# A gated scan and feed-forward kernel: interleaved head rows, state products in two column parts, and a planner with other transfer costs

## The chip, the cores and the metric

The kernel runs on one core of one Trainium2 chip. The metric is device time of one execution in microseconds (us), the median of several runs. A difference of about 0.2% is what these runs can tell from no change.

## What is computed

Per batch (4) and head (8) a complex state of 48 x 48 is carried over 768 steps: it is decayed by a complex gate, a product of key and value is added, and the query reads its real part. Then every token goes through a feed-forward block with a quadratic unit in between.

```python
mag = np.sqrt(a_re * a_re + a_im * a_im)
scale = np.minimum(mag, 0.999) / (mag + 1e-06)
for t in range(S):
    new_re = ar * S_re - ai * S_im
    new_im = ar * S_im + ai * S_re
    S_re, S_im = (new_re + kv, new_im)
    y[:, :, t] = np.einsum('bhd,bhde->bhe', q[:, :, t], S_re)
...
h = x @ w_in                                       # 3072 x 384 by 384 x 2048
g = np.where(pos, h, np.where(neg, 0.0, (h + beta) ** 2 / (4.0 * beta)))
return (g @ w_out).astype(np.float32)
```

## The kernel before

**Units and blocks.** The 4 x 768 tokens are cut into 12 units of 256 tokens (`U`); a batch is three units. Two units make a block; there are six blocks. Per block the feed-forward part (`moe`) works on 512 tokens: 16 steps `f`, each with 9 matmuls into `h` (L951) and, three steps later, 9 into the outputs `o` (L1026); in between ACT and DVE form `s`, `g`, `gh` and `gl`. Each product of two float32 values is made of three fast matmuls, of a high part with a high part, a low part with a high part and a high part with a low part.

**Gates.** `gates(u)` computes, on DVE and ACT alone, the running sum of the logarithm of the gate's size and of its angle along the tokens (scans at L544 and L571). Key and query (`kq`) are scaled by it (L561) and multiplied by the cosine into `x` and by the sine into `kq` itself (L647, the helper `turn`). In these tiles the partitions are rows of several heads.

**Spreading the heads.** The matmuls want all 96 rows of one head (48 cosine, 48 sine) in one tile. `spread` moves them by DMAs from SBUF to SBUF into three head tiles, `hd0` to `hd2`, with five transfers for the cosine rows and five for the sine rows of a unit: 48, 48, 32, 16 and 16 partitions. The order of the rows in `x` comes from `key_rows`, which the host uses to lay out the inputs: 48 rows of one head, then 48 of another, and so on; the cosine rows go to partitions 0 to 47 of the head tile, the sine rows to 48 to 95. There is one set of head tiles for all units but unit 1.

**Attention.** `attend(u)` takes a unit as two chunks of 128 tokens and makes, per chunk: scores (`sc`, L791, masked by DVE into `am`, L799), transposes of the keys (`tp`, L737, copied by ACT to `kT`), state products (`dp`, L764: per head one matmul of 128 tokens, 96 columns of `kT` loaded, 48 columns of values moving; DVE adds them to the state `st`, L774 and L776), and values (`yp`, L830 from the state, L838 from `am`: two heads go side by side into columns 0 to 63 and 64 to 127 of the array). ACT copies `yp` to `xr` and `ys`, and six small DMAs (`xr<-ys`) bring the rest rows of a block into place before the block is split into `xH` (ACT, L921) and `xL` (DVE, L928).

These steps are put together in *visits*: the parts of one visit follow each other on PE without anything between, and the first of them waits for the inputs of all. Per chunk the visits are: values of the chunk before and both groups of scores; then state products of the chunk before and transposes. The last visit of a unit has state products, then values.

**Weights.** Each of 16 weight tiles comes packed (`raw_i`, `raw_o`) and is unpacked by three DVE instructions (L377, L386, L395) and an ACT cast to the high part (L401). The low part is a DVE subtraction (L406), but for the first `LO_PE` = 4 tiles it is made by PE (L415, L416) and copied by ACT (L430).

**The order of the work.** Every operation is recorded with an engine, a cost, its reads and writes and perhaps a due time (`Plan.op`). `Plan.order` then plays the plan with these numbers: each engine takes, among the operations that are ready, the one due first. The result is written out engine by engine and not changed at run time. A DMA costs `DMA_ISSUE` = 70 ns of SP, starts 1500 ns later, moves 260 bytes per ns one after the other, and its end is seen 900 ns later. All DMAs are issued by SP, in one order; each uses one of eight semaphores in turn, and waits until the transfer that had it before is finished. Attention of the units of block `b + 1` is due in a stretch of the feed-forward part of block `b`, given by `WINDOW` (and `EARLY` for the first). Units 0, 1 run before the first feed-forward part. Where PE would stand idle in the start, `warm` adds matmuls without use (`idle`, L1075).

Of the kernel before, what the change touches and what calls it, by code (L numbers as in the profile page):

```python
# [20 lines left out]
NH = 8  # L21
S = 768
D = 48
DM = NH * D
DFF = 2048
# [30 lines left out]
LAG = 3  # L56
HOLD = {'DVE': (0.3, 20000.0), 'ACT': (0.3, 20000.0)}
WINDOW = (0.05, 0.7)
EARLY = (0.05, 0.6)
HEAD = ((15000, 8000), (8000, 2000))  # L60
# [3 lines left out]
WARM = 0.75  # L64
ABS_ACT = 5
LO_PE = 4
INFLATE = 1.6
# [40 lines left out]
class Plan:  # L108
# [42 lines left out]
    def order(self):  # L151
# [8 lines left out]
        for i in range(n - 1, -1, -1):  # L160
            eng, cost, _, _, d, dma = ops[i]
            t = big if d is None else d
            if dma:
                own = DMA_FIX + DMA_END + dma / DMA_BW + 600
# [11 lines left out]
        avail = {e: [] for e in free}  # L176
        dma_free = 0.0

# [9 lines left out]
        while done < n:  # L188
# [105 lines left out]
def gated_scan_moe(  # L294
# [55 lines left out]

    def dma(nbytes, dst, src, r=(), w=(), due=None):
        return pl.op(
            "SP", DMA_ISSUE, lambda: nc.sync.dma_start(dst(), src()), r=r, w=w, dma=nbytes, due=due  # L353
        )
# [9 lines left out]
    def weights(n, kind, i, slot):  # L364
# [7 lines left out]
        N = 2 * DM  # L372
        pl.op("SP", DMA_ISSUE, lambda: load(k, RAW.get()), w=[RAW], dma=P * N * 8)
        pl.op(
# [60 lines left out]
    def ranges(k):  # L435
        RAW = tl(turn_of("g", 4), [P, 2 * DM, 2], U32, f"chk_{k}")
        top, low = (lambda: RAW.get()[:, :, 1]), (lambda: RAW.get()[:, :, 0])
        N = 2 * DM
        pl.op("SP", DMA_ISSUE, lambda: load(k, RAW.get()), w=[RAW], dma=P * N * 8)
# [26 lines left out]
    def gates(u):  # L466
# [158 lines left out]
        if u == 1:  # L625
# [3 lines left out]
                    "hd_1",  # L629
                    lambda t, n=n: t[: 2 * D, : 2 * n * U].rearrange(  # L630
                        "p (j e n) -> p j e n", j=n, e=2
# [4 lines left out]
        else:  # L636
            hd = [
                tl(f"hd{g}", [2 * D, n, 2, U], F32, f"hd_{u}_{g}")
                for g, n in enumerate((3, 3, 2))
            ]  # L640
# [16 lines left out]
        def spread(g, e, t):  # L657
            r = D * e
            h = hd[g]
            row = 2 * U * 4  # L660
            if g < 2:
                dma(
                    D * NJ * row,
                    lambda: h.get()[r : r + D],
                    lambda: t.get()[g * D : (g + 1) * D],
                    r=[t],
                    w=[(h, e)],
                )
            else:
                dma(  # L670
                    64 * row,
                    lambda: h.get()[r : r + 32],
                    lambda: t.get()[2 * D :, 0:2],
                    r=[t],
                    w=[(h, (e, 0))],
                )
                for q in range(2):
                    p = 2 * D + 16 * q
                    dma(
                        16 * row,  # L680
                        lambda q=q: h.get()[r + 32 : r + D, q],
                        lambda p=p: t.get()[p : p + 16, 2],
                        r=[t],
                        w=[(h, (e, 1 + q))],
                    )
# [13 lines left out]
    def attend(u):  # L699
# [28 lines left out]
        def transposes(c):  # L728
            cs = slice(c * CH, (c + 1) * CH)
            out = []  # L730
            for g in range(2):
                TP = bank([P, 4, 2 * D], f"tp_{u}_{g}_{c}")
                KT = tl(turn_of("kT", 2), [P, 4, 2 * D], F32, f"kT_{u}_{g}_{c}")

                def run(g=g, TP=TP):
                    for i, h in enumerate(GROUPS[g]):
                        PE_.transpose(  # L737
                            TP.get()[:, i, :], head(h)[:, 0, cs], ident[: 2 * D, : 2 * D]
                        )

                def tail(TP=TP, KT=KT):
                    pl.op(
                        "ACT",
                        act(8 * D, psum=True),
                        lambda: A_.copy(KT.get(), TP.get()),
# [8 lines left out]
        def products(c):  # L754
            kT = carry.pop("kT")
            DP = bank([2 * D, NH, D], f"dp_{u}_{c}")
            V_c = carry["V"]
            old = carry.get("st")
            ST = tl(turn_of("st", 3), [2 * D, NH, D], F32, f"st_{u}_{c}")
            carry["st"] = ST  # L760

            def run():
                for i in range(NH):
                    PE_.matmul(  # L764
                        DP.get()[:, i, :],
                        kT[i // 4].get()[:, i % 4, :],
                        V_c[0].get()[:, V_c[1], i * D : (i + 1) * D],
                        start=True,
                        stop=True,
                    )  # L770

# [6 lines left out]

            return [(NH * pe32(D), run, [*kT, V_c[0]], DP, tail)]

# [108 lines left out]
        if part == 0:  # L889
            carry.pop("st", None)  # L890
            carry.pop("kT", None)
        for c in range(NC):
# [5 lines left out]
            if part * NC + c < S // CH - 1:  # L898
                second = second + transposes(c)
            if second:  # L900
                visit(second)
            carry["V"] = (V, c)
        last = values(NC - 1, *pending)
        if part < NPART - 1:
            last = products(NC - 1) + last
        visit(last)
# [451 lines left out]
```

## Time and profile before

| | |
|---|---|
| runs shown | 600.36, 600.93, 600.93 us; median 600.93 |
| profiled execution | 598.38 us, span of its instructions 596.6 us |
| granted TensorE clock, mean | 0.982 |
| first feed-forward matmul starts at | 86.34 us |
| last feed-forward matmul starts near | 589 us |

The profile is of one execution. Its rows name a line of the kernel, an engine, an operation and the tiles (out<-in) with their shapes and counts. In the profile a float32 matmul of the attention part counts as two, as PE makes two passes of it; the fast matmuls of the feed-forward part count as one. PEld is the load of a matmul's stationary operand. A matmul's duration includes its way through the array, so in a row of matmuls the pace is read from the starts, not from the durations. SPq is SP issuing DMAs.

### The profile page before, as it was taken

How to read it: one execution, taken by the hardware profiler on the slowest of the kernel's cores; microseconds unless marked ns; L12 is line 12 of the kernel's file. 1: busy time of each engine (PE TensorE's matmuls, PEld its weight loads, DVE VectorE, ACT ScalarE, POOL GpSimd, SP SyncE). 2: the span in 40 equal slices, each digit the busy share in tenths (PEclk: the TensorE clock that was granted, in tenths of full speed). 3: DMA queues.
4: the chain of work that ended last, by engine and by line, in shares of the span. 5: the costliest groups of instructions: out<-in, count | busy, mean ns of one | idle time of the engine just before them, and what ended most of it. 6: DMA issues, size and time to landing. Idle time of an engine off the chain costs nothing.

```text
span 596.6 us, 9075 instructions
## 1 busy us (share of the span) xinstructions
PE 560.9 (94%) x3502; PEld 474.5 (80%) x3502; DVE 449.0 (75%) x636; ACT 392.6 (66%) x632; POOL 1.4 (0%) x16
## 2 busy tenths in 40 slices
PE   5378979999999999999999999999999999999995
PEld 5167968888688888888888888888888888888884
DVE  3999979989979899688697687887785444555552
ACT  8658769988887775666756576566567577543332
POOL 0000000000000000000000000000000000000000
PEclk9599989999999999999999999999999999999998
DMA  8379573673381540540710640710765956010001
GB/s 350 125 186 233 162 194 115 175 276 103 105 213 45 107 134 0 136 152 18 181 60 1 145 148 13 190 48 11 175 217 183 236 200 213 13 55 0 1 0 57
DMA packets 21794, 74.18 MB, mean 124 GB/s; under 512 B 3889, under 2 KB 8497, under 8 KB 21745
## 3 DMA queue, kind: packets, MB, share of 16 engines
q1 hardware_dynamic: 21744, 73.55, 42.2%
q8 instruction: 28, 0.46, 0.3%
q14 instruction: 22, 0.17, 0.1%
HBM read 48.76 MB, written 4.72 MB: 90 GB/s over the span
## 4 chain that ended last, share of the span: by engine, by line
PE 66%; DVE 15%; ACT 7%; DMA 7%; SPq 2%; issue 2%; DVEq 0%; ACTq 0%
PE o L1026 26%; PE h L951 26%; PE sc L791 5%; DMA hd<-kq 4%; PE dp L764 3%; PE yp L830 2%; PE yp L838 2%; ACT ai L500 2%; SPq L353 2%; PE tp L737 2%; DVE x L647 1%; DVE ai L571 1%; ACT x L500 1%; DVE kq L561 1%; DVE g L995 1%
## 5 line engine op out<-in xcount | busy, mean ns | idle before, releaser
L951 PE MATMUL h<-xH,wi 128*128 128x512 f32 x576 | 181.6, 396 | 0.9 <-DVE g L995 0.8
L1026 PE MATMUL o<-gh,wo 128*128 128x512 f32 x576 | 178.9, 392 | 0.1
L1026 PEld LDWEIGHTS o<-gh,wo 128*128 128x128 f32 x576 | 107.2, 188 | 23.1 <-issue 0.7
L951 PEld LDWEIGHTS h<-xH,wi 128*128 128x128 f32 x576 | 105.4, 189 | 22.7 <-DVE g L995 2.1
L995 DVE TENSOR_TENSOR g<-h,s 128x512 f32<-128x512 f32 x96 | 65.9, 687 | 67.3 <-ACT s L976 57.0
L1026 PE MATMUL o<-gl,wo 128*128 128x512 f32 x288 | 112.3, 390 | 1.2 <-DVE gl L1013 1.2
L951 PE MATMUL h<-xL,wi 128*128 128x512 f32 x288 | 112.2, 390 | 0.0
L1009 ACT CAST gh<-g 128x512 fp32r<-128x512 f32 x96 | 59.6, 621 | 70.7 <-DVE g L1003 66.7
L976 ACT ACTIVATE s<-h,cst 128x512 f32<-128x512 f32 x96 | 65.8, 687 | 42.4 <-PE h L951 38.8
L1013 DVE TENSOR_TENSOR gl<-g,gh 128x512 fp32r<-128x512 f32 x96 | 66.1, 689 | 31.4 <-ACT gh L1009 30.7
L1026 PEld LDWEIGHTS o<-gl,wo 128*128 128x128 f32 x288 | 54.1, 188 | 13.2 <-DVE gl L1013 1.7
L951 PEld LDWEIGHTS h<-xL,wi 128*128 128x128 f32 x288 | 54.1, 188 | 11.5
L500 ACT ACTIVATE ai<-ai 128x768 f32<-128x768 f32 x53 | 44.6, 845 | 21.7 <-DMA ai<-in_ari_dram 8.0
L1003 DVE SCALAR_TENSOR_TENSOR g<-s,g 128x512 f32<-128x512 f32 x80 | 55.4, 692 | 2.7
L791 PE MATMUL sc<-hd 96*128 96x128 f32 x384 | 50.3, 283 | 5.1 <-DMA hd<-kq 4.6
L791 PEld LDWEIGHTS sc<-hd 96*128 96x128 f32 x384 | 46.4, 194 | 9.4 <-DMA hd<-kq 5.6
L838 PE MATMUL yp<-am,V 128*64 128x128 f32 x384 | 35.5, 273 | 0.0
L799 DVE TENSOR_TENSOR am<-sc,mask 128x512 f32<-128x512 f32 x48 | 32.0, 684 | 3.9 <-PE sc L791 3.7
L830 PE MATMUL yp<-hd,st 96*64 96x128 f32 x320 | 32.1, 278 | 0.0
L764 PEld LDWEIGHTS dp<-V,kT 128*96 128x96 f32 x320 | 30.1, 165 | 1.8
L500 ACT ACTIVATE x<-x 128x768 f32<-128x768 f32 x24 | 20.3, 846 | 15.0 <-DVE x L544 14.7
L764 PE MATMUL dp<-V,kT 128*96 128x48 f32 x320 | 29.6, 245 | 0.0
(86 smaller groups left out, 629.5 us busy)
## 6 DMA issues: line engine op xcount, KB each, us to landing
chk<-in_wl_dram SPq DMA_DIRECT2D x16, 768.0 KB, 4.4
kq<-in_kq_dram SPq DMA_DIRECT2D x12, 768.0 KB, 5.1
ai<-in_ari_dram SPq DMA_DIRECT2D x11, 768.0 KB, 6.0
hd<-x SPq DMA_DIRECT2D x24, 288.0 KB, 5.1
hd<-kq SPq DMA_DIRECT2D x24, 288.0 KB, 5.8
raw_i<-in_wl_dram SPq DMA_DIRECT2D x8, 768.0 KB, 7.7
raw_o<-in_wl_dram SPq DMA_DIRECT2D x8, 768.0 KB, 4.4
V<-in_v_dram SPq DMA_DIRECT2D x12, 384.0 KB, 4.0
```

The source lines that it names most:

```text
L500: lambda: A_.activation(out(), src(), f, **kw),
L764: PE_.matmul(DP.get()[:, i, :], kT[i // 4].get()[:, i % 4, :], V_c[0].get()[:, V_c[1], i * D : (i + 1) * D], start=True, stop=True,)
L791: PE_.matmul(SC.get()[:, i, :], t[:, 0, cs], t[:, 1, cs], start=True, stop=True)
L830: PE_.matmul(o, st.get().rearrange("p h e -> p (h e)")[:, lo : lo + 64], head(h)[:, 1, cs], start=True, stop=False,)
L838: PE_.matmul(o, V.get()[:, c, lo : lo + 64], ams[g].get()[:, 2 * pr + e, :], start=st is None, stop=True,)
L951: PE_.matmul(H.get(), weight["i", f // 2].get()[:, f % 2, part, sl], x.get()[:, j, :], start=j == 0 and n == 0, stop=j == NJ - 1 and n == 2,)
L976: lambda: A_.activation(SS.get(), H.get(), AF.Relu, bias=c_half, scale=-0.5 if spare else 0.5),
L995: lambda: V_.tensor_tensor(G.get(), H.get(), SS.get(), op=ALU.max),
L1003: lambda: V_.scalar_tensor_tensor(G.get(), SS.get(), 1.0, G.get(), op0=ALU.min, op1=ALU.mult),
L1009: pl.op("ACT", act(T), lambda: A_.copy(GH.get(), G.get()), r=[G], w=[GH])
L1013: lambda: V_.tensor_tensor(GL.get(), G.get(), GH.get().bitcast(F32), op=ALU.subtract),
L1026: PE_.matmul(PO[m].get(), weight["o", f // 2].get()[:, f % 2, part, sl], g.get(), start=f == 0 and n == 0, stop=f == NF - 1 and n == 2,)
```

## The change

1. `key_rows` lays the rows of two heads alternately (row 2d of one head, row 2d + 1 of the other), and `spread` takes every second partition of the source and writes every second partition of the head tile, so that cosine and sine rows alternate there. Sizes and numbers of the transfers are the same; `SPREADS` = 0 leaves all of them on SP.
2. A state product is made in two matmuls per head, of columns 0 to 63 and 64 to 95 of `kT`.
3. The visits: per chunk first values and state products of the chunk before and the first group of scores, then the second group of scores and the transposes. The last visit of a unit has values, then state products.
4. The planner: an issue costs 470 ns, the rate is 410 bytes per ns for loads (`LOAD`) and 240 for head transfers (`MOVE`), a transfer starts 2400 ns after its issue, its end is seen 50 ns later, and the eight semaphores in turn are modelled (`LANES`).
5. Numbers: `WINDOW` and `EARLY` begin at 0 instead of 0.05, `ABS_ACT` 3 instead of 5 (an absolute value of units 3 and 4 moves from ACT to DVE), `LO_PE` 5 instead of 4.

```diff
-DMA_FIX, DMA_END, DMA_BW, DMA_ISSUE = 1500, 900, 260.0, 70
+DMA_FIX, DMA_END, DMA_ISSUE, LANES = 2400, 50, 470, 8
+LOAD, MOVE = 410.0, 240.0
...
-ABS_ACT = 5
-LO_PE = 4
+ABS_ACT = 3
+LO_PE = 5
...
-        out += [(j, d) for d in range(D)] + [(NJ + j, d) for d in range(D)]
+        out += [(h, d) for d in range(D) for h in (j, NJ + j)]
...
-                b = max(t + DMA_FIX, dma_free)
-                dma_free = b + dma / DMA_BW
-                end[i] = dma_free + DMA_END
+                q = queue.setdefault(eng, [0.0] * LANES)
+                t = max(t, q[-LANES])
+                q.append(max(t + DMA_FIX, q[-1]) + dma)
+                end[i] = q[-1] + DMA_END
+                start[i] = t
+                free[eng] = t + cost
...
-                    lambda: h.get()[r : r + D],
-                    lambda: t.get()[g * D : (g + 1) * D],
+                    lambda: h.get()[e:HR:2],
+                    lambda: t.get()[g : 2 * D : 2],
...
-                    PE_.matmul(
-                        DP.get()[:, i, :],
-                        kT[i // 4].get()[:, i % 4, :],
-                        V_c[0].get()[:, V_c[1], i * D : (i + 1) * D],
+                    for a, z in ((0, 64), (64, HR)):
+                        PE_.matmul(
+                            DP.get()[a:z, i, :],
+                            kT[i // 4].get()[:, i % 4, a:z],
+                            V_c[0].get()[:, V_c[1], i * D : (i + 1) * D],
...
-            return [(NH * pe32(D), run, [*kT, V_c[0]], DP, tail)]
+            return [(NH * 124, run, [*kT, V_c[0]], DP, tail)]
...
-            first = [] if pending is None else values(c - 1, *pending)
+            before = [] if pending is None else values(c - 1, *pending) + products(c - 1)
             sc, ams = scores(c)
-            visit(first + sc)
-            second = products(c - 1) if c else []
+            tp = transposes(c) if state_after(c) else []
+            if before:
+                visit(before + sc[:1])
+                visit(sc[1:] + tp)
```

The plan orders every engine anew. Three places follow; numbers behind the names count tiles, and `L` is the line in the kernel before or after. On PE, from unit 2's first scores to the first feed-forward matmul, before:

```order
L791 MATMUL sc_1_0_684<-hd_2_589 128x128 x2
L737 MATMUL tp_0_0_694<-ident,hd_0_585 128x96
L737 MATMUL tp_0_0_694<-ident,hd_1_587 128x96
...
L737 MATMUL tp_1_0_700<-ident,hd_2_589 128x96 x2
L951 MATMUL h_0_708<-xH_682,wi_160 128x512 x2
L951 MATMUL h_0_708<-xL_692,wi_160 128x512
...
L764 MATMUL dp_0_838<-V_486,kT_0_0_706 96x48 x4
L764 MATMUL dp_0_838<-V_486,kT_1_0_719 96x48 x4
```

and in the change, at the same place:

```order
L756 MATMUL tp_1_0_750<-ident,hd_2_607 128x96 x2
L1095 MATMUL idle<-mask,ident 128x128 x2
L848 MATMUL yp_0_767<-hd_0_603,st_1_729 64x128
L848 MATMUL yp_0_767<-hd_1_605,st_1_729 64x128
L856 MATMUL yp_0_767<-am_0_0_739,V_569 64x128 x2
...
L782 MATMUL dp_0_792<-V_569,kT_0_0_755 64x48
L782 MATMUL dp_0_792<-V_569,kT_0_0_755 32x48
...
L809 MATMUL sc_0_1_812<-hd_0_603 128x128
L809 MATMUL sc_0_1_812<-hd_1_605 128x128
L971 MATMUL h_0_822<-xH_788,wi_138 128x512 x2
```

The values, the state products (now in pairs of 64 and 32 columns) and half of the next scores of unit 2 stand ahead of the first `h`, where before they stood behind it.

On SP, from unit 2's sine transfers to the transfers of block 0's rest rows, before:

```order
L353 DMA hd_0_585<-kq_329 48x1536
L353 DMA hd_1_587<-kq_329 48x1536
L353 DMA hd_2_589<-kq_329 32x1024
L353 DMA hd_2_589<-kq_329 16x512 x2
L353 DMA xr_389<-ys_391 16x512 x6
L353 DMA kq_649<-in_kq_dram 128x1536
```

and in the change:

```order
L363 DMA hd_0_603<-kq_374 48x1536
L363 DMA hd_1_605<-kq_374 48x1536
L363 DMA hd_2_607<-kq_374 32x1024
L363 DMA hd_2_607<-x_336 16x512
L363 DMA hd_2_607<-kq_374 16x512 x2
L363 DMA kq_716<-in_kq_dram 128x1536
L363 DMA xr_448<-ys_450 16x512 x6
```

The load of unit 3's `kq` is now issued ahead of the six `xr` transfers.

On DVE, up to the turn of unit 2 (`x` and `kq`, lines 647 and 660), before:

```order
L591 SCALAR_TENSOR_TENSOR ai_230<-ai_230 128x768
L406 TENSOR_TENSOR wo_479<-raw_o_210,wo_479 128x2x384
L386 SCALAR_TENSOR_TENSOR raw_i_296<-raw_i_296,y_i_453 128x768
L799 TENSOR_TENSOR am_0_1_553<-sc_0_1_539,mask 128x512
L799 TENSOR_TENSOR am_1_1_566<-sc_1_1_547,mask 128x512
L647 TENSOR_TENSOR x_309<-kq_329,ai_230 128x1536
L776 TENSOR_TENSOR st_0_583<-st_1_475,dp_0_556 96x384
L647 TENSOR_TENSOR kq_329<-kq_329,ai_230 128x1536
```

and in the change:

```order
L605 SCALAR_TENSOR_TENSOR ai_273<-ai_273 128x768
L817 TENSOR_TENSOR am_0_0_558<-sc_0_0_488,mask 128x512
L817 TENSOR_TENSOR am_1_0_561<-sc_1_0_494,mask 128x512
L794 TENSOR_TENSOR st_1_571<-st_0_465,dp_1_541 96x384
L660 TENSOR_TENSOR x_336<-kq_374,ai_273 128x1536
L660 TENSOR_TENSOR kq_374<-kq_374,ai_273 128x1536
L400 SCALAR_TENSOR_TENSOR raw_i_252<-raw_i_252,y_i_499 128x768
```

Counted over all instructions ahead of unit 2's `x`, four are fewer in the change: one L386, two L799 and one L406. Ahead of unit 0's `x` stand two more, the L386 and L395 of the second weight.

More of the change, by code (lines that the diff above doesn't have):

```diff
@@ L23 @@
 D = 48
+HR = 2 * D
 DM = NH * D
@@ L56 @@
 LAG = 3
+SPREADS = 0
+SPREAD = ("SP", "ACT")
 HOLD = {'DVE': (0.3, 20000.0), 'ACT': (0.3, 20000.0)}
-WINDOW = (0.05, 0.7)
-EARLY = (0.05, 0.6)
+WINDOW = (0.0, 0.7)
+EARLY = (0.0, 0.6)
 HEAD = ((15000, 8000), (8000, 2000))
@@ L349, in gated_scan_moe, with dma @@
     V_, A_, PE_ = nc.vector, nc.scalar, nc.tensor
-    def dma(nbytes, dst, src, r=(), w=(), due=None):
+    def dma(nbytes, dst, src, r=(), w=(), due=None, rate=LOAD, eng="SP"):
+        queue = {"SP": nc.sync, "ACT": nc.scalar, "POOL": nc.gpsimd}[eng]
         return pl.op(
-            "SP", DMA_ISSUE, lambda: nc.sync.dma_start(dst(), src()), r=r, w=w, dma=nbytes, due=due
+            eng,
+            DMA_ISSUE,
+            lambda: queue.dma_start(dst(), src()),
+            r=r,
+            w=w,
+            dma=nbytes / rate,
+            due=due,
         )
@@ L372, in weights @@
         N = 2 * DM
-        pl.op("SP", DMA_ISSUE, lambda: load(k, RAW.get()), w=[RAW], dma=P * N * 8)
+        pl.op("SP", DMA_ISSUE, lambda: load(k, RAW.get()), w=[RAW], dma=P * N * 8 / LOAD)
         pl.op(
@@ L438, in ranges @@
         N = 2 * DM
-        pl.op("SP", DMA_ISSUE, lambda: load(k, RAW.get()), w=[RAW], dma=P * N * 8)
+        pl.op("SP", DMA_ISSUE, lambda: load(k, RAW.get()), w=[RAW], dma=P * N * 8 / LOAD)
         pl.op(
@@ L637, in gates @@
             hd = [
[L638 to L639 removed]
+                tl(f"hd{g}", [HR, n, 2, U], F32, f"hd_{u}_{g}") for g, n in enumerate((3, 3, 2))
             ]
```

50 lines of the change are left out of this document (27 added, 23 removed).

## The prediction

> **What bounds the kernel now.** I read the busy shares first, then stages by windows, then the chain of waits in the start, then groups by line for durations. The page's first part shows TensorE (PE) far ahead of the others:
>
> ```profile
> PE 560.9 (94%) x3502; PEld 474.5 (80%) x3502; DVE 449.0 (75%) x636; ACT 392.6 (66%) x632; POOL 1.4 (0%) x16
> ```
>
> The windows (start and end, length, then busy time of PE, PE's weight loads, DVE, ACT, POOL) split the span at the first matmul of the feed-forward part (86.3), around one hole (160 to 164) and at the last (589.2):
>
> ```profile
> 0.00:86.30 86.30, 60.37 (x500) 53.28 (x501) 70.88 (x92) 62.26 (x94) 1.36 (x16) 0.91 0.70 201
> 86.30:160.00 73.70, 73.54 (x467) 62.02 (x466) 70.82 (x101) 64.63 (x102) 0.00 (x0) 1.00 0.52 172
> 160.00:164.00 4.00, 2.53 (x9) 1.28 (x8) 4.00 (x5) 3.97 (x6) 0.00 (x0) 1.00 0.16 29
> 164.00:180.00 16.00, 15.80 (x82) 13.06 (x82) 11.57 (x16) 13.96 (x24) 0.00 (x0) 1.00 0.86 221
> 180.00:420.00 240.00, 240.00 (x1540) 204.04 (x1539) 198.09 (x283) 155.76 (x243) 0.00 (x0) 1.00 0.32 87
> 420.00:589.20 169.20, 168.56 (x912) 140.82 (x911) 93.31 (x141) 91.46 (x167) 0.00 (x0) 1.00 0.36 111
> 589.20:596.60 7.40, 0.13 (x3) 0.02 (x2) 0.29 (x2) 0.59 (x2) 0.00 (x0) 0.70 0.36 115
> ```
>
> From 86.3 to 589.2 PE is busy 500.4 of 502.9 us, so there the time is the sum of PE's instructions, and 1 us less of them is 1 us less time. Before 86.3 PE waits for the first units. Between the two, from 86.3 to 160, DVE is 96% busy (70.82 of 73.70): PE is full, but with a second engine right behind it. The span is 596.6, the profiled execution took 598.38, and the median of the runs shown is 600.93, 2.55 more; I carry that difference along.
>
> **The state products (dp).** The rows by line give the loads, the timeline the pace:
>
> ```profile
> L764 PEld LDWEIGHTS dp<-V,kT 128*96 128x96 f32 x320 | 30.1, 165 | 1.8
> L791 PEld LDWEIGHTS sc<-hd 96*128 96x128 f32 x384 | 46.4, 194 | 9.4 <-DMA hd<-kq 5.6 <-issue 1.9 <-ACT kT L745 1.1
> L838 PEld LDWEIGHTS yp<-am,V 128*64 128x64 f32 x384 | 23.6, 136 | 1.2 <-issue 1.1
> ```
>
> ```profile
> 189.12 1.48 PE L764 MATMUL dp<-V,kT 128*96 128x48 f32 x16
> 190.44 0.84 PE L737 MATMUL tp<-ident,hd 96*128 96x96 f32 x8
> 191.06 0.71 PE L951 MATMUL h<-xH,wi 128*128 128x512 f32 x2
> ...
> 195.94 1.48 PE L764 MATMUL dp<-V,kT 128*96 128x48 f32 x16
> 197.35 0.44 PE L830 MATMUL yp<-hd,st 96*64 96x128 f32 x4
> 197.62 0.39 PE L838 MATMUL yp<-am,V 128*64 128x128 f32 x4
> 197.84 0.39 PE L830 MATMUL yp<-hd,st 96*64 96x128 f32 x4
> ...
> 198.94 0.39 PE L838 MATMUL yp<-am,V 128*64 128x128 f32 x4
> 199.26 0.73 PE L951 MATMUL h<-xH,wi 128*128 128x512 f32 x2
> ...
> 215.71 1.95 PE L791 MATMUL sc<-hd 96*128 96x128 f32 x16
> 217.42 0.70 PE L951 MATMUL h<-xH,wi 128*128 128x512 f32 x2
> ```
>
> Every matmul in float32 is two passes. A dp of one chunk (8 heads, 16 passes) runs from 189.12 to 190.44: 1.32, or 82 ns a pass, though only 48 columns move; 16 passes of the scores, with 128 columns moving, take 215.71 to 217.42, 107 ns a pass. So dp is held by its load of 96 columns, and a load grows by about 29 ns for 32 columns (136, 165, 194 for 64, 96, 128). The values (yp) are two matmuls of 64 columns side by side: four passes in 0.22 (197.62 to 197.84), 110 for two, against 107 for one pass of the scores with as much to move. Two column parts there run at the same time.
>
> The change cuts each head's dp into columns 0 to 63 and 64 to 95. If these run side by side as in yp, a pair of passes is held by the 64-column load: 82 - 29 = 53, plus the 3 that yp's pair shows over one pass, 56. I take 60, a little above, since no row has loads of unequal width together: 16 x 0.060 = 0.96 per chunk, 0.36 less. If they don't overlap, 56 + 29 gives 85 per pair, as now. The ends are thus 53 (0.46 less per chunk) and no gain; what would be worse is a rival below. How many chunks lie in the full stretch, by the windows of that line alone (16 passes a chunk):
>
> ```profile
> 0.00:86.20 86.20, 5.95 (x64) 5.88 (x64) 0.91 0.70 201
> 86.20:589.20 503.00, 23.68 (x256) 24.21 (x256) 1.00 0.38 111
> ```
>
> 256 passes are 16 chunks: 16 x 0.36 = **5.8 us** (0 to 7.4). The other 4 lie in the start, where PE waits anyway.
>
> **The start.** Unit 2's scores stand ahead of the first feed-forward matmul; they wait for unit 2's ten head transfers, and these for DVE's turn of x:
>
> ```profile
> 69.98 1.75 DVE L647 TENSOR_TENSOR x<-kq,ai 128x1536 f32<-128x1536 f32 x1
> ```
>
> ```profile
> 71.76 3.82 SPq L353 DMA_DIRECT2D hd<-x  x5
> 75.68 4.60 SPq L353 DMA_DIRECT2D hd<-kq  x5
> 80.37 3.69 SPq L353 DMA_DIRECT2D xr<-ys  x6
> ```
>
> ```profile
> 82.75 2.60 PE L791 MATMUL sc<-hd 96*128 96x128 f32 x14 [0.22 <-DMA hd<-kq]
> 86.34 1.03 PE L951 MATMUL h<-xH,wi 128*128 128x512 f32 x2
> ```
>
> SP issues from 71.76 on without a gap, 0.03 after the turn ends (69.98 + 1.75 = 71.73), and PE goes on when the last transfer has landed, at 82.75: 11.0 after the turn. In the new order DVE has four instructions less ahead of that turn: one L386, two L799 and one L406, which now stand behind it or, in the case of L406, are done by PE and ACT:
>
> ```profile
> L799 DVE TENSOR_TENSOR am<-sc,mask 128x512 f32<-128x512 f32 x48 | 32.0, 684 | 3.9 <-PE sc L791 3.7
> L386 DVE SCALAR_TENSOR_TENSOR raw_i<-raw_i,y_i 128x768 uint32<-128x768 uint32 x8 | 7.6, 954 | 0.1
> L406 DVE TENSOR_TENSOR wo<-raw_o,wo 128x768 fp32r<-128x768 f32 x7 | 6.7, 951 | 0.0
> 30.00:60.00 30.00, 25.14 (x198) 21.28 (x198) 28.93 (x37) 20.97 (x33) 0.00 (x0) 1.00 0.90 211
> ```
>
> That is 0.95 + 2 x 0.68 + 0.95 = 3.3, on an engine busy 28.93 of 30 us; back to back they overlap a little, so 2.9. The data is there at 79.8. From then the old order needs scores and transposes; the new one also puts values (197.35 to 199.26: 1.9), a dp (0.96) and half the scores (0.86) ahead of the first feed-forward matmul: 1.71 + 0.62 + about 0.5 for DVE's mask product + 1.9 + 0.96 + 0.86 = 6.55, hence 86.35. That is the old time, with 3.7 of PE's work done before it that used to come after. I take **3.0 us**, because SP now issues unit 3's kq load ahead of the six xr transfers, and behind it everything waits if its buffer is still being read. The ends: that load stands 2.5 us longer and nothing comes sooner, 2 lost; transfers land sooner as well and the hole at 160 closes, 6 gained.
>
> On the speed of the transfers the rows say that one of a head group, of 288 KB takes 5.8 us to land, a load of 768 KB 5.1:
>
> ```profile
> kq<-in_kq_dram SPq DMA_DIRECT2D x12, 768.0 KB, 5.1
> hd<-kq SPq DMA_DIRECT2D x24, 288.0 KB, 5.8
> ```
>
> The Trainium skill, SBUF — State Buffer, section on the DMA port swizzle, says that bandwidth depends on how many of the 16 ports the partitions reach; by its formula 48 rows in a line from 0 reach 8, every second of 96 all 16, so the movement itself would halve and the start's term be about 4 instead of 3. Nothing in the rows shows it yet, and the ten issues (8.5 us) hold the last landing anyway.
>
> **Small edits.** One more weight's low part goes from DVE (L406, 0.95) to PE and ACT in the start, where PE has room; the absolute value of units 3 and 4 goes from ACT to DVE, two instructions of about 0.56 by the row below, in the stretch where DVE is 96% busy. These two nearly cancel on DVE: 0, at most 1.1 late if ACT isn't what waits.
>
> ```profile
> L610 DVE TENSOR_SCALAR ai<-ai 128x768 uint32<-128x768 uint32 x7 | 3.9, 555 | 0.2
> ```
>
> The dp after the values needs no more switches of shape than before: each unit still enters and leaves the 64-column form twice. Transfers planned otherwise: 0 from 180 on, since PE covers everything; a transfer would have to be late by more than the planner's slack.
>
> **The sum.** 598.38 - 5.8 - 3.0 = 589.6 for a profiled execution, and 600.93 - 8.8 = **592.1 us** for the median.
>
> **Rivals.** *DVE keeps the end of the first block.* For: 96% busy there, and PE's one hole in the full stretch ends on it:
>
> ```profile
> 161.14 0.73 PE L1026 MATMUL o<-gh,wo 128*128 128x512 f32 x2
> 163.11 0.50 PE L1026 MATMUL o<-gl,wo 128*128 128x512 f32 x1 [1.24 <-DVE gl L1013]
> ```
>
> If DVE gets there no sooner, PE's 3.0 and four chunks' 1.4 are given back: 600.93 - 4.4 = 596.5. Against: some of DVE's 15.4 idle us before 86.3 are filled by the new order. Chance 0.15.
>
> *The parts don't overlap.* Then dp stays at 1.32 and only the start gains: 597.9. Chance 0.07.
>
> *Slower: 64 and 32 columns are two shapes, and PE empties itself at each change.* Price by rows: into the 64-column form, dp would end at 195.94 + 1.32 = 197.26, yp starts 0.09 later and its first group takes 0.27 for 0.22: 0.14. Out of it, the next matmul starts 0.10 late (199.26 for 198.94 + 0.22). The new dp changes width 15 times per chunk: 15 x 0.10 to 0.14 = 1.5 to 2.1 on top of 1.32, times 16 chunks 24 to 34, less 3.0: 622 to 632. It turns the result slower as soon as one change costs over 0.013 (240 changes against the start's 3.0). No row of before alternates widths; yp's pairs, of equal width, pay nothing. The Trainium skill, TensorEngine Tiling (Array Packing), Key Properties, speaks for it: changing the tiling mode, not just the tile, drains TensorE, and it lists 128x64 and 128x32 as two modes; by it this rival would be the result. Against it stand only the yp rows, where a second part in free columns costs 3 ns. Chance 0.13.
>
> That the change doesn't do what it says can be left out: the order of instructions shows each part.
>
> **How the numbers follow.** Forecast 0.63, rivals 0.15, 0.07, 0.13; 0.02 for something not thought of. The forecast alone spans 600.93 - 7.4 - 6 = 587.5 to 600.93 - 5.8 + 2 = 597.1. With the two milder rivals, and the start lost as well in the second (about 601), and another 1.5 below for the hole at 160, the range is 586 to 601. About 0.2% (1.2 us) is what a measurement of this kernel can tell from no change: faster 0.84, same 0.03, slower 0.13.
>
> **What would show it.** Right: dp at 0.9 to 1.05 per chunk in the timeline; the x turn of unit 2 ending near 69; the first feed-forward matmul near 86 with a yp and a dp of unit 2 ahead of it; PE without holes from 180. Wrong: a dp above 1.3; a wait of several us for DVE before block 1 (the first rival); yp or dp rows with gaps of 0.1 between passes (the third).

## The result: 636.24 us, slower by 5.9%

The changed kernel takes 636.24 us (634.64 to 636.85, 4 runs), the kernel before 600.64 (599.67 to 600.93, 4 runs): ratio 1.059, 95% interval 1.057 to 1.062. The forecast was 592.1. It went as the third rival said (64 and 32 columns are two shapes), and beyond the 632 of its range. The profiled execution took 636.85 us, its span is 635.1, the mean granted clock 0.983, about the 0.982 of before.

The page's first part after (busy time and share of each engine): PE has 51.1 us more, and DVE, ACT and POOL have what they had.

```profile
PE 612.0 (96%) x3874; PEld 509.3 (80%) x3874; DVE 451.8 (71%) x637; ACT 391.2 (62%) x632; POOL 1.4 (0%) x16
```

The timeline of PE after, at one chunk in the full stretch (start, duration, engine, line, operation; a step's cost is read from its start to the start of the next row):

```profile
208.92 0.39 PE L856 MATMUL yp<-am,V 128*64 128x128 f32 x4
209.14 3.60 PE L782 MATMUL dp<-V,kT 128*64 128x48 f32 x32
212.66 0.72 PE L971 MATMUL h<-xH,wi 128*128 128x512 f32 x2
```

One chunk's state products take 3.52 us (212.66 - 209.14), where one matmul per head took 1.32 and the forecast had 0.96.

The windows after, split at the first feed-forward matmul (the columns are start and end, length, busy time of PE, its loads, DVE, ACT, POOL, then the granted clock):

```profile
0.00:98.97 98.97, 84.25 (x688) 72.08 (x689) 74.70 (x97) 67.51 (x103) 1.36 (x16) 0.93 0.60 198
98.97:627.20 528.23, 527.51 (x3188) 437.17 (x3186) 376.82 (x538) 323.01 (x529) 0.00 (x0) 1.00 0.32 102
```

Two parts are late. The start ends at 98.97 for 86.34, 12.6 later. Behind it PE works 527.5 us for 500.4, 27.1 more, with 0.7 us of holes (time in which PE stands idle) for 2.5. The start's part too begins with dp, as DVE's timeline after shows at unit 2's turn of x (the bracket is the idle time ahead, and who ended it):

```profile
72.59 0.55 DVE L794 TENSOR_TENSOR st<-st,dp 96x384 f32<-96x384 f32 x1 [2.31 <-PE dp L782]
73.07 1.75 DVE L660 TENSOR_TENSOR x<-kq,ai 128x1536 f32<-128x1536 f32 x1
```

DVE stands 2.31 us before that turn because the state's addition, queued ahead of it, waits for a dp; the turn begins at 73.07 where I had forecast its end near 69. And one more dp of 3.6 us stands right ahead of the first feed-forward matmul, as PE's timeline shows:

```profile
94.53 3.60 PE L782 MATMUL dp<-V,kT 128*64 128x48 f32 x32
98.06 1.16 PE L809 MATMUL sc<-hd 96*128 96x128 f32 x8
98.97 0.48 PE L971 MATMUL h<-xH,wi 128*128 128x512 f32 x1
```

### The profile page after: what moved, and what is told of

Same layout as the page of the kernel before. It is cut to its first block, busy times and chain, and to the rows that moved or that the text cites. A ratio compares the mean times of both kernels' runs of the same rounds, so it can differ in the third digit from the quotient of the medians.

```text
span 635.1 us, 9847 instructions
## 1 busy us (share of the span) xinstructions
PE 612.0 (96%) x3874; PEld 509.3 (80%) x3874; DVE 451.8 (71%) x637; ACT 391.2 (62%) x632; POOL 1.4 (0%) x16
## 4 chain that ended last, share of the span: by engine, by line
PE 89%; DVE 6%; ACT 2%; DMA 1%; issue 0%; ACTq 0%; DVEq 0%
PE o L1046 31%; PE h L971 31%; PE dp L782 11%; PE sc L809 7%; PE yp L856 3%; PE yp L848 3%; PE tp L756 2%; ACT ai L514 1%; DVE kq L575 1%; ACT x L514 1%; DVE x L558 1%; DVE ai L585 1%; DVE raw_i L400 1%; DVE x L660 1%; DMA ai<-in_ari_dram 1%
## 5 line engine op out<-in xcount | busy, mean ns | idle before, releaser
L971 PEld LDWEIGHTS h<-xH,wi 128*128 128x128 f32 x576 | 106.7, 189 | 22.1 <-DVE g L1015 0.9
L782 PE MATMUL dp<-V,kT 128*32 128x48 f32 (+1 forms) x640 | 72.0, 227 | 0.0
L782 PEld LDWEIGHTS dp<-V,kT 128*32 128x32 f32 (+1 forms) x640 | 53.6, 121 | 17.7
L514 ACT ACTIVATE ai<-ai 128x768 f32<-128x768 f32 x51 | 42.8, 842 | 33.0 <-DVE ai L530 11.4
L809 PEld LDWEIGHTS sc<-hd 96*128 96x128 f32 x384 | 48.3, 196 | 5.0 <-DMA hd<-kq 2.7
L1095 PEld LDWEIGHTS idle<-mask,ident 128*128 128x128 f32 x226 | 30.4, 213 | 2.6 <-POOL mask masks.py:66 1.7
L1095 PE MATMUL idle<-mask,ident 128*128 128x128 f32 x226 | 30.8, 297 | 1.7 <-POOL mask masks.py:66 1.7
```

What stands on the lines that cost most here:

```text
L514: lambda: A_.activation(out(), src(), f, **kw),
L782: PE_.matmul(DP.get()[a:z, i, :], kT[i // 4].get()[:, i % 4, a:z], V_c[0].get()[:, V_c[1], i * D : (i + 1) * D], start=True, stop=True,)
L809: PE_.matmul(SC.get()[:, i, :], t[:, 0, cs], t[:, 1, cs], start=True, stop=True)
L971: PE_.matmul(H.get(), weight["i", f // 2].get()[:, f % 2, part, sl], x.get()[:, j, :], start=j == 0 and n == 0, stop=j == NJ - 1 and n == 2,)
L1095: PE_.matmul(idle["h1"], ident, mask, start=True, stop=True)
```

## The experiments

The theory: PE empties itself at each change between a matmul of 64 and one of 32 columns, and the new dp changes 15 times per chunk. The rival: two small instructions per head cost what they cost, in any order and any width. Four kernels tell these apart; then come the parts of the rest of the change. All times of the kernel before beside them are 598.8 to 599.75, so ratios are given.

### The split undone (e1)

```diff
-                    for a, z in ((0, 64), (64, HR)):
+                    for a, z in ((0, HR),):
```

> The changed kernel with the state product of a head in one matmul of 96 columns again; order, transfers and planner costs stay those of the changed kernel. Both theories: a chunk's dp goes back from 3.53 us to 1.32. 16 chunks in the full stretch give 16 x 2.21 = 35.4, the 4 in the start up to 8.8 more: 592 to 601 us. What is left against the kernel before (600.6) is the worth of everything else in the change; if it comes out above 603, something besides the split is late too.

Measured: 599.8 us, ratio 1.001 (0.998 to 1.004). The timeline of PE:

```profile
190.99 0.39 PE L856 MATMUL yp<-am,V 128*64 128x128 f32 x4
191.31 1.56 PE L782 MATMUL dp<-V,kT 128*96 128x48 f32 x16
192.69 0.71 PE L971 MATMUL h<-xH,wi 128*128 128x512 f32 x2
```

1.38 us per chunk. Ahead of it stands one thing more: from the last values to the first state product e1 takes 0.32 (191.31 - 190.99), the changed kernel 0.22 (209.14 - 208.92), since e1 changes there from 64 columns to 96 and the changed kernel stays at 64. So e1's step costs 1.48 beside the 3.52. The split alone is worth the whole loss, 36.4 us, and all the rest of the change together is worth nothing. That second half I had not expected, and it is taken up below.

### One change of width, or seven, in place of fifteen (e2, e8)

In e2 all eight parts of 64 columns of a chunk come first, then all eight of 32; in e8 the order is 64, 64, 32, 32 for every two heads. The instructions are the same 16.

```diff
-                for i in range(NH):
-                    for a, z in ((0, 64), (64, HR)):
+                for a, z in ((0, 64), (64, HR)):
+                    for i in range(NH):
```

> The same 16 matmuls of a chunk's state products, but all eight parts of 64 columns first and then all eight of 32. Theory (each change between the 64- and 32-column forms empties PE, about 0.14 us): one change inside a chunk instead of 15, so dp is near 3.53 - 14 x 0.14 = 1.6 us (1.4 to 1.9) and the time 636.2 - 20 x 1.9 = 598 (594 to 606). Rival (two small instructions per head cost 0.22 each whatever their order): dp stays at 3.5 and the time at 636.

> The changed kernel's two parts of 64 and 32 columns, in the order 64, 64, 32, 32 for every two heads: 7 changes of width inside a chunk, between the 15 of the changed kernel (3.53 us per chunk) and the 1 of the grouped order (1.73). Theory (each change costs the same, 1.80 / 14 = 0.129): 1.73 + 6 x 0.129 = 2.50 us per chunk, and 604.8 + 20 x 0.77 = 620 (616 to 622). Rival (the price lies in the first change of a visit or in the pairing of one head's parts): 1.7 or 3.5 us per chunk, 605 or 636.

Measured: 604.76 us (ratio 1.009, 1.006 to 1.011) and 617.22 (1.029, 1.023 to 1.036). PE's timeline in e2:

```profile
196.75 1.88 PE L782 MATMUL dp<-V,kT 128*64 128x48 f32 x32
198.56 0.73 PE L971 MATMUL h<-xH,wi 128*128 128x512 f32 x2
```

and in e8:

```profile
201.07 2.61 PE L786 MATMUL dp<-V,kT 128*64 128x48 f32 x32
203.61 0.73 PE L975 MATMUL h<-xH,wi 128*128 128x512 f32 x2
```

So a chunk takes 1.81 us with one change, 2.54 with seven, 3.52 with fifteen: (2.54 - 1.81) / 6 = 0.122 and (3.52 - 2.54) / 8 = 0.122. The three lie on a line, so the price is one of each change, **0.12 us**, and not of the instruction. The rival falls. The line also gives what is left without any change inside the chunk: 1.81 - 0.12 = 1.69. The starts of the single passes in e2's trace say what that is: 16 passes of 64 columns 58 ns apart and 16 of 32 columns 42.5 ns apart, one after another (1.61 together), and 0.09 for the change out into `h`. In e2 neighbours lie in the same columns, so it has no pair that could run side by side. In the changed kernel the two parts of a head lie in different columns, and still its first pass of 32 starts 0.151 us behind the last of 64, where the two parts of e4 (below) start 0.007 apart. So parts of unequal width didn't run side by side, and what is left stands above the 1.38 of one matmul per head. The Trainium skill, TensorEngine Tiling (Array Packing), Key Properties, says that changing the tiling mode, not just the tile, drains TensorE; these runs agree, at 0.12 us a change.

### Equal widths (e3, e4)

e3 cuts the 96 columns in three parts of 32. e4 cuts them in two of 64: the second takes 32 columns of the next head along (GpSimd zeroes 32 columns behind the last head of a tile), and 32 rows of its result are not read.

```diff
-                    for a, z in ((0, 64), (64, HR)):
+                    for a, z in ((0, 32), (32, 64), (64, HR)):     # e3
+                    for a, z in ((0, 64), (64, P)):                # e4
```

> The state product of a head in three parts of 32 columns each (0, 32, 64), no 64-column part. Theory (the change of width costs, not the number of instructions): no change of width inside a chunk; 48 passes of 32 columns, side by side in threes 0.8 us, one after another at about 0.04 1.9 us, and the time 582 to 606. Rival (an instruction costs 0.22 by itself): 24 x 0.22 = 5.3 us per chunk, the time 636 + 20 x 1.75 = 671.

> The state product of a head in two parts of 64 columns, 0 to 63 and 64 to 127; columns 96 to 127 are the next head's first 32 (behind the last head of a tile, 32 columns that GpSimd sets to zero), and the 32 rows of the result that belong to them are not read. Theory (only a change of width empties PE): the pair runs side by side as the values do, 53 to 60 ns a pass, 0.85 to 0.96 us per chunk, and the time 636.2 - 20 x 2.6 = 584 to 593. Rival (two small instructions per head cost 0.22 each): dp 3.5, time 636. A third: equal widths, but no overlap of the two: 32 x 0.055 = 1.8 us per chunk, 602.

Measured: e3 595.53 us (ratio 0.994, 0.991 to 0.997), e4 597.68 (0.997, 0.994 to 1.000). PE's timeline in e3:

```profile
192.22 0.88 PE L782 MATMUL dp<-V,kT 128*32 128x48 f32 x48
193.04 0.74 PE L971 MATMUL h<-xH,wi 128*128 128x512 f32 x2
```

and in e4:

```profile
196.54 1.09 PE L790 MATMUL dp<-V,kT 128*64 128x48 f32 x32
197.56 0.74 PE L979 MATMUL h<-xH,wi 128*128 128x512 f32 x2
```

0.82 us per chunk with 48 passes, 1.02 with 32: more instructions than the changed kernel's or as many, and less than a third of its time. Parts of equal width do run side by side, and my 0.96 for two parts was near for that case. Both kernels also go from one place in the array to another at each matmul, so it is the change of width that costs, not the change of place. But e4's time missed its range: PE works 5.1 us less than in e1 behind the first feed-forward matmul, and its holes there grow from 5.3 to 9.0 us. The windows of e1, then of e4:

```profile
86.38:590.29 503.91, 498.57 (x2949) 418.96 (x2947) 375.17 (x540) 325.94 (x532) 0.00 (x0) 0.99 0.34 108
```

```profile
89.68:592.13 502.45, 493.49 (x3185) 413.73 (x3186) 376.22 (x542) 326.59 (x535) 3.54 (x28) 0.99 0.35 109
```

Hole time is length less PE's busy time: 503.91 - 498.57 = 5.3, 502.45 - 493.49 = 9.0. These windows are of one execution each, and that of e4 was the slowest of its ten, 601.66 us, with the first feed-forward matmul at 89.68 for 86.38. So they show that holes ate most of the gain in that execution, and not how much of it in the median.

### The split, and the three parts, in the kernel before (e12, e5)

The same two edits in the kernel before, with its own order and costs.

```diff
+                    for a, z in ((0, 64), (64, 2 * D)):               # e12
+                    for a, z in ((0, 32), (32, 64), (64, 2 * D)):     # e5
                         PE_.matmul(
-                            DP.get()[:, i, :],
+                            DP.get()[a:z, i, :],
```

> The kernel before with only its state products cut into 64 and 32 columns; nothing else. Theory (the whole loss is the 15 changes of width per chunk, whatever the order): dp 3.5 us per chunk, 16 x 2.2 to 20 x 2.2 = 35 to 44 more, 635 to 644. Rival (the loss needs the new order, where the values stand right ahead of the state products): under 620.

> The kernel before, with only its state products cut into three 32-column parts; order and planner costs stay. Theory (parts of equal width run side by side, and a change of width costs some 0.12 us each way): dp 0.8 us of passes and two changes of 0.12 for 1.32 per chunk, 0.3 to 0.6 less, over 16 to 20 chunks 5 to 12 us: 588 to 596. Rival (the gain of the three-part kernel of the changed order came from the order, not the parts): 599 to 602. If other engines set the pace where PE becomes shorter, holes appear behind 160 and the time stays above 594.

Measured: e12 642.78 us (ratio 1.072, 1.066 to 1.078), e5 594.64 (0.991, 0.988 to 0.994). The price of the split doesn't need the new order. PE's timeline in e12:

```profile
207.15 3.65 PE L765 MATMUL dp<-V,kT 128*64 128x48 f32 x32
210.73 0.62 PE L831 MATMUL yp<-hd,st 96*64 96x128 f32 x4
```

3.58 us per chunk. The loss, 42 to 44, is more than 16 x (3.58 - 1.32) = 36: the chunks in the start count as well, and the first feed-forward matmul begins 4.0 later, at 90.34. The rest is the clock: behind the start it stands at 0.50 four times for 3.4 us, each time right behind such a dp or at its end (last section), which loses another 6.8 us of work. Less 1.8 us of holes (0.6 for 2.5), that makes 45.2, and the two spans differ by 45.1 (641.7 - 596.6).

### The alternating rows, undone and alone (e7, e13)

e7 is e1 with the rows as before; e13 is the kernel before with nothing but the alternating rows. Order and costs stay in both.

```diff
-                    lambda: h.get()[e:HR:2],                   # e1 to e7
-                    lambda: t.get()[g : 2 * D : 2],
+                    lambda: h.get()[D * e : D * e + D],
+                    lambda: t.get()[g * D : (g + 1) * D],
...
-                    lambda: h.get()[r : r + D],                # before to e13
-                    lambda: t.get()[g * D : (g + 1) * D],
+                    lambda: h.get()[e : 2 * D : 2],
+                    lambda: t.get()[g : 2 * D : 2],
```

> The changed kernel with dp in one matmul, and with the head rows laid out as before: 48 cosine rows, then 48 sine rows, in place of alternating ones. Order and planner costs stay. Theory (rows spread over all partitions land sooner, 3.9 us for 5.1 in the two traces): the 288 KB transfers take 5.1 to 5.8 again, and the first feed-forward matmul stands 0 to 1.5 us later than 86.4, for the ten issues hide part of it: 599.8 to 602. Rival (the transfers are shorter because of their order, not their rows): 3.9 us stays, time the same.

> The kernel before with only the head rows alternating; order and dp as before. Theory (alternating rows let the head transfers land sooner, 3.9 to 4.9 us for 5.1 to 5.8, and in the start PE and ACT wait for them): the turn of unit 2's x stands 1 to 3 us sooner than 69.98, the first feed-forward matmul 2 to 4 sooner than 86.34, and the time 595 to 598, as far as holes behind it don't give it back. Rival (the old order hides the transfers; the rows pay only in the new order, where they were worth 7): 599 to 601.

Measured: e7 607.15 us (ratio 1.011, 1.005 to 1.016), e13 595.43 (0.993, 0.991 to 0.996). The rows are worth 6 to 7 us in the new order (1.011 less 1.001 as ratios, 607.15 less 599.8 as times) and 4.2 in the old one. Read the other way, e7 is the new order with its planner and its small edits, and neither the split nor the rows: by itself that is 1.1% slower than the kernel before, with the first feed-forward matmul at 92.76 and 9.5 us of holes behind it. So "worth nothing" in e1 is a gain from the rows and a loss of about the same size from the rest; no run parts the order from the planner's transfer costs and the small edits. The page's list of transfers (size, median us from issue to landing), for before, then the changed kernel, e7 and e13:

```profile
hd<-x SPq DMA_DIRECT2D x24, 288.0 KB, 5.1
hd<-kq SPq DMA_DIRECT2D x24, 288.0 KB, 5.8
```

```profile
hd<-x SPq DMA_DIRECT2D x24, 288.0 KB, 3.9
hd<-kq SPq DMA_DIRECT2D x24, 288.0 KB, 5.1
```

```profile
hd<-x SPq DMA_DIRECT2D x24, 288.0 KB, 5.2
hd<-kq SPq DMA_DIRECT2D x24, 288.0 KB, 5.9
```

```profile
hd<-x SPq DMA_DIRECT2D x24, 288.0 KB, 3.8
hd<-kq SPq DMA_DIRECT2D x24, 288.0 KB, 5.0
```

A transfer lands 0.7 to 1.3 us sooner wherever the rows alternate. The Trainium skill, SBUF — State Buffer, section on the DMA port swizzle, makes bandwidth depend on how many ports the partitions reach; the runs agree in direction. No run separates the number of ports from other effects of the alternation. What it saves is shown by the starts of unit 2's turn of x and of the first feed-forward matmul. In e1:

```profile
67.90 1.76 DVE L660 TENSOR_TENSOR x<-kq,ai 128x1536 f32<-128x1536 f32 x1 [0.64 <-ACT ai L514]
86.38 0.71 PE L971 MATMUL h<-xH,wi 128*128 128x512 f32 x2
```

in e7, the same order with the old rows:

```profile
71.68 1.76 DVE L660 TENSOR_TENSOR x<-kq,ai 128x1536 f32<-128x1536 f32 x1 [0.67 <-ACT ai L514]
92.76 0.71 PE L971 MATMUL h<-xH,wi 128*128 128x512 f32 x2
```

and in e13, the old order with the new rows:

```profile
69.52 1.75 DVE L647 TENSOR_TENSOR x<-kq,ai 128x1536 f32<-128x1536 f32 x1
83.53 0.73 PE L951 MATMUL h<-xH,wi 128*128 128x512 f32 x2 [0.80 <-ACT xH L921]
```

In the old order the turn gains 0.5 us (69.98 before), less than the 1 to 3 I expected, and the way from it to the feed-forward part 2.3 more (83.53 - 69.52 = 14.0 for 16.4). In the new order the old rows put the turn 3.8 later, which already stands behind unit 1's transfers, and the first feed-forward matmul 6.4 later. My expectation of 0 to 1.5 for e7 missed by far: three units' transfers follow each other in the start, and the delay of each is passed on. Against e1, unit 0's first issue comes at the same time (35.02 for 35.05), unit 1's sine transfers 2.3 later (53.63 for 51.28), unit 2's first 3.8 later (73.46 for 69.68).

### What the planner is told (e6, e9, e10, e11), and the two gains together (e14)

Only the cost of a chunk's state products changes: e6 and e11 are e3 with 760 and 840 ns, e9 is e1 with 1360, e10 is e4 with 1048, all in place of 992. e14 is e5 with alternating rows.

```diff
-            return [(NH * 124, run, [*kT, V_c[0]], DP, tail)]
+            return [(NH * 95, run, [*kT, V_c[0]], DP, tail)]     # e6; 105, pe32(D) = 170 and 131 in e11, e9 and e10
```

> The changed kernel with three 32-column parts, and with the planner told 760 ns for a chunk's state products in place of 992, near the 0.82 us that the trace of the three-part kernel shows. Theory (the holes of 8.6 us behind the first feed-forward matmul there come from a plan that puts ACT's and DVE's work too late for the faster PE): holes shrink to 3 to 5 us, 590 to 593. Rival (the holes are ACT's and DVE's own shortage there, whatever the plan): 594 to 598, as the three-part kernel with the old cost (595.5).

> The changed kernel with dp in one matmul, and with the planner told 1360 ns for a chunk's dp (the cost that the kernel before had), in place of 992; the trace shows 1.40. Theory (a cost that fits keeps ACT's and DVE's work in step with PE; in the one-matmul kernel with 992 the holes behind the first feed-forward matmul were 5.3 us, with the granted clock at 0.5 for some us behind one of them): holes 1 to 3 us and no low clock, 594 to 597 us, so everything but the split is worth 3 to 6. Rival (the rest of the change is worth nothing, whatever the plan): 599 to 601.

> The kernel with two parts of 64 columns, told 1048 ns per chunk in place of 992; the trace shows 1.06. Theory (the cost told makes the plan fit): holes 9.0 to 2 or 4 us, 591 to 594. Rival (992 fitted as well as 1048 does, and 9.0 us of holes came all the same, so the holes are a matter of which plan comes out): anything from 590 to 600, no order by fit.

> The kernel with three 32-column parts, told 840 ns per chunk, between 760 (589.7 us) and 992 (595.5). Theory (the fit decides: 0.82 us of passes, so 840 fits as well as 760): 589 to 592, which would be 1.4 to 2% faster than the kernel before. Rival (each plan falls out by chance): 592 to 598.

> The kernel before with alternating rows and the state products in three 32-column parts; order and the planner's costs as before. Theory (the two gains lie at different places, the start and the full stretch, and add): 594.6 less what the rows alone are worth in the old order, 590 to 593. Rival (behind 160 DVE and ACT set the pace once PE is shorter): 593 to 596.

| run | kernel | us | ratio, 95% interval |
|---|---|---|---|
| e3 | three parts, told 992 | 595.53 | 0.994 (0.991 to 0.997) |
| e11 | three parts, told 840 | 593.14 | 0.989 (0.985 to 0.993) |
| e6 | three parts, told 760 | 589.74 | 0.986 (0.980 to 0.991) |
| e9 | one matmul, told 1360 | 600.63 | 1.003 (1.000 to 1.005) |
| e10 | two parts of 64, told 1048 | 601.01 | 1.003 (1.000 to 1.005) |
| e14 | before, three parts, alternating rows | 591.21 | 0.987 (0.984 to 0.991) |

The windows of e3, then of e6, from the first feed-forward matmul on:

```profile
87.69:584.71 497.02, 488.39 (x3428) 407.03 (x3427) 374.88 (x541) 324.93 (x533) 0.00 (x0) 1.00 0.35 110
```

```profile
89.88:579.34 489.46, 487.26 (x3429) 407.27 (x3427) 373.05 (x537) 324.21 (x531) 0.00 (x0) 1.00 0.35 111
```

PE's work is the same within 1.1 us; the holes are 8.6 in e3 and 2.2 in e6. So the plan decides whether a shorter dp is kept. But that a cost near the truth makes the better plan is not borne out: e9 and e10 were told what the trace shows, and e9 came out no better than e1, e10 worse than e4 by its median (single executions of both lie between 595 and 602); e11, told the nearest to the 0.82 of its trace, lies above its range and behind e6. What decides between plans stays open. e6 and e14 are the fastest of all kernels here; e14 shows that the gains of the rows and of the equal parts add, within the noise (595.43 and 594.64 alone, 591.21 together).

## Why the prediction was wrong, point by point

**The state products.** The step that failed is the pace of a pair: "a pair of passes is held by the 64-column load ... I take 60, a little above, since no row has loads of unequal width together". The row it was taken from, the values, has pairs of equal width, and e4 shows the step right for that case: 1.02 us per chunk for 0.96. With unequal widths there is no pair at all: 1.69 for the passes one after another and the way out, and 15 changes at 0.122 on top, 3.52. The sum had -5.8 for 16 chunks; behind the start there are 15 in the changed kernel, the windows of that line show (480 passes, 32 to a chunk, and 160 ahead of it), and 15 x (3.52 - 1.48) = 30.6 is what they cost more than in e1. PE's busy time there differs by 28.9 (527.51 - 498.57): to a lower clock e1 loses 3.4 us of work, the changed kernel 1.7 (last section), and 30.6 + 1.7 - 3.4 = 28.9.

```profile
0.00:98.97 98.97, 17.99 (x160) 13.41 (x160) 0.93 0.60 198
98.97:627.00 528.03, 53.97 (x480) 40.23 (x480) 1.00 0.32 102
```

**The third rival** had the mechanism and its place, and a price of 0.10 to 0.14 that holds the measured 0.122. It came out low, 622 to 632, for two reasons: it set the 15 changes on top of 1.32, not of 1.69, and it let the start keep its 3.0, where five chunks are late as well and the first feed-forward matmul stands 12.6 behind that of e1. The 0.13 I gave it was too little: the only row against it, that of the values, has one width, so it says nothing on a change of width, and the two rows at the borders of the values, from which I took the price, spoke for it.

**The start.** With dp in one matmul the numbers came true: unit 2's turn ends at 69.7 (67.90 + 1.76) where I had "near 69", the first feed-forward matmul begins at 86.38 for 86.35, and PE has less to do behind it: 498.57 for 500.4 in e1, 497.01 in e7 at full clock, where I had 3.7 less. The reason was wrong: "DVE has four instructions less ahead of that turn" doesn't bring it forward, since e7 has the same four less and its turn begins 1.7 later than before. It was the rows, which I had put at 1 of 4 us, "the ten issues hold the last landing anyway". The issues became shorter too: in e1 SP's ten take 7.0 us for 8.5. So that these numbers fit is luck: one term too large stood in for one too small.

**"0 from 180 on, since PE covers everything"** was wrong as well, and this is why the rest of the change is worth nothing. e1 gains 1.8 us of PE work behind the start (5.2, had the low clock not taken 3.4) and loses 2.9 in holes (5.3 for 2.5), the waits of PE in e1 behind the start (us in total, times, longest) being these:

```profile
PE h L971 <- DVE g L1015: 3.6, 3, 2.2
PE dp L782 <- ACT kT L762: 1.7, 1, 1.7
```

The second, in the timeline of ACT and PE in e1:

```profile
484.91 0.62 ACT L1029 CAST gh<-g 128x512 fp32r<-128x512 f32 x1 [0.50 <-DVE g L1023]
485.44 0.85 ACT L762 COPY kT<-tp 128x384 f32<-128x384 f32 x2
...
485.96 1.89 PE L782 MATMUL dp<-V,kT 128*96 128x48 f32 x16 [1.72 <-ACT kT L762]
```

The dp of the new visit follows the values at once and waits for ACT's copy of the keys. The keys' transposes start at 479.44, but ACT's queue has other work ahead of the copy: from 479.93 on four passes over weights that the last block loads once more (`chk`), the first of which waited 1.65 us for its load, and then `gh`. In the changed kernel the long dp hides nearly all of this. The plan is the same in e1, e2, e8 and the changed kernel, and the holes behind the start are 5.3 us at 1.38 per chunk (e1), 5.3 at 1.81 (e2), 3.5 at 2.54 (e8) and 0.7 at 3.52.

**The first rival** (DVE keeps the end of the first block) couldn't come where dp is long: the hole of before at 161 to 163 is gone in the changed kernel. Where dp is short, 3.6 us of e1's waits are put down to DVE's g, but the longest, the 2.2 us ahead of the `h` at 447.21, isn't DVE's own lateness, and it lies far behind the first block:

```profile
445.74 1.27 ACT L996 ACTIVATE s<-h,cst 128x512 f32<-128x512 f32 x2 [1.88 <-DMA out_dram<-ob]
446.46 0.69 DVE L1015 TENSOR_TENSOR g<-h,s 128x512 f32<-128x512 f32 x1 [3.39 <-ACT s L996]
```

DVE stood idle for ACT's `s`, and ACT for the store of the block before: `s` and the output tile `ob` take turns in the same three buffers, so a faster PE runs into the landing of an output, 5.1 us after its issue at 440.65. So the engine of this rival was wrong too, as far as that hole goes.

**The second** (no overlap, dp stays at 1.32) had half of it: there is no overlap, but without it dp is 1.69 before any change of width, not 1.32.

## What to carry to other kernels

In these runs each change of a matmul's column width on PE cost 0.12 us, and equal widths ran side by side. So cut a product into parts of one width, or put all parts of one width together, and count the changes of width before counting passes. A row in which pairs of one width run side by side is no evidence for pairs of two widths; where no row of a trace shows the combination, a test of the step by itself comes before the sum. And an engine that is full hides the lateness of the others: what it saves is kept only as far as their queues, and the transfers they wait for, are early enough at that place. A wait is followed back past the first engine it names.

## What the runs showed of the hardware that was not expected

- Three parts of 32 columns are faster than two of 64: 0.82 us per chunk for 1.02, though each head takes six passes in place of four. About half of that difference is given back ahead of it: from the last values, which are 64 wide, to dp e3 takes 0.32 and e4 0.22.
- Behind a hole, and behind a dp of changing widths, the clock can fall to a half. The windows of e1 at 484 to 496, with the granted clock as the last column but two:

```profile
484.00:486.00 2.00, 0.28 (x7) 0.04 (x2) 1.28 (x3) 1.50 (x5) 0.00 (x0) 1.00 0.94 353
486.00:488.00 2.00, 2.00 (x18) 2.00 (x19) 0.30 (x2) 1.86 (x4) 0.00 (x0) 0.76 0.64 246
488.00:490.00 2.00, 2.00 (x10) 1.90 (x10) 1.34 (x2) 0.80 (x1) 0.00 (x0) 0.50 0.10 43
...
492.00:494.00 2.00, 2.00 (x6) 1.56 (x5) 0.49 (x1) 1.20 (x4) 0.00 (x0) 0.54 0.32 77
```

  A hole of 1.7 us is followed by some 6.8 us at 0.50 (from the 0.76 and 0.54 of the slices at its ends), so up to 3.4 us of work are lost behind it, more than the hole itself. Another hole of e1, 2.2 us near 446, is followed by full clock. The trace's record of the granted clock shows one difference between them: in e1 its changes come at multiples of 3.41 us from each other. Counted in such stretches from the fall at 487.04, the hole of 1.7 lies in one stretch (483.63 to 487.04, PE busy 1.69 of 3.41), and that of 2.2 is cut by a border at 446.08 (busy 2.34 and 2.28). No run tries this on purpose.

- No hole is needed. In e12 PE is busy throughout, and the clock falls right behind the dp of 207.15 to 210.73:

```profile
207.50:210.90 3.40, 3.40 (x32) 2.50 (x33) 3.23 (x3) 1.66 (x2) 0.00 (x0) 0.99 0.00 0
210.90:214.30 3.40, 3.40 (x33) 3.07 (x31) 1.02 (x2) 0.00 (x0) 0.00 (x0) 0.51 0.09 17
```

  The same comes at 296.2, 347.4 and 501.0 in e12 and at 446.8 in the changed kernel, each time for 3.4 us and behind a dp that nearly fills the 3.41 us ahead of the fall (28 to 30 of its 32 passes start there). Behind the other dp in the full stretch of both kernels, of which at most 28 passes start in one such stretch, the clock stays full. So the changes of width cost their 0.12 us each and, behind 5 of 31 dp there, 1.7 us of clock.
